# Decode attention beside a feed-forward: K loaded in pairs of tiles into two large buffers, V tile by tile into two others

## Chip, cores and metric

The kernel runs on one core of one Trainium2 chip. The metric is device time in microseconds (us) of one execution: 2529.17 us, the median of three runs (2528.84 to 2529.18). A DMA issue below is one instruction on the SP (SyncE) queue that moves one block from HBM to SBUF over the core's 16 DMA engines.

## Reference

One token `x` (512 numbers) goes through attention with a long cache and through a gated feed-forward, and a scalar gate mixes the two:

```python
g = sigmoid((x * gate_w).sum(-1))
q = (x @ wq)                                  # 32 heads of 128
scores = einsum("bhqd,bhkd->bhqk", q, k_cache) * 128 ** -0.5   # 65536 keys a head
a = einsum("bhqk,bhkd->bhqd", softmax(scores), v_cache) @ wo   # 4096 -> 512
b = (silu(x @ w_gate) * (x @ w_up)) @ w_down  # 512 -> 1792 -> 512
return g * a + (1 - g) * b
```

All inputs are bf16. `k_cache` and `v_cache` are 32 x 65536 x 128 each, 1.07 GB together; everything else is about 14 MB. Each cache entry is read once.

## The kernel before

**Tiles.** A head's 65536 keys are cut into G = 4 tiles of 16384 keys; over 32 heads that makes N = 128 K tiles and 128 V tiles. A tile is 128 partitions by 128 keys by 128 numbers, 32 KB a partition and 4 MB in all. Within a tile partition p holds 128 consecutive keys, so its 32 KB are one contiguous run in HBM (L110). `ring` has five slots of 32 KB a partition (L17, L81). `take` hands out the slot that has been free longest, `give` returns it; K, V, `wq`, the feed-forward's weights and the last half of `wo` all pass through these five. A load into a slot waits until the last reader of its earlier contents has finished.

**Queries.** All 32 heads' q are made at the start: 32 matmuls (L147) with `x` spread over 128 columns give q copied to all partitions, and ScalarE stores it as `q_bc` (L154).

**One K tile.** VectorE multiplies the tile by q (L245, in place) and halves the width by adding (L249): from 128 to 64 in the first G tiles, to 32 after those (`width_of`). TensorE finishes the sum over the remaining columns with matmuls by the identity into `S_ps` (`scores`, L258: 16 matmuls in the first four tiles, 8 after). VectorE sums the last four (`fold`, L272). After four tiles of a head, `row_max` (L278 to L282) and `exponentials` (L287 to L291) turn the scores into `P_sb`. In the first tile of each head the multiplication and the additions are done in two halves so that these small steps can go between.

**One V tile.** `values` (L313): 32 matmuls of 128x512 into `O_ps`. After a head's four V tiles, `head_turn` (L342, L349) brings the result into a column of `oT`, and `project` (L356) adds that head's row of `wo`. `wo` comes in four blocks of four heads (L161) along the way for heads 0 to 15, and in four pieces behind the last V tile (L167) for heads 16 to 31.

**Order.** The order on each engine is written out by hand (`manual_schedule`, the list `steps` at L397 and the loop at L408). Each step loads one K tile and one V tile (L410, L415), multiplies one K tile, runs `values` for one V tile and then `scores` for the K tile. V runs behind K by up to LAG = 8 tiles. All cache loads are issued on SP in the order of the loop, and SP stands still at a load whose slot is not free. The last V tile is loaded in six pieces (`V_CUTS`), and its last 8 key columns go through `head_turn` directly (L334).

Of the kernel before, what the change touches and what calls it, by code (L numbers as in the profile page):

```python
# [11 lines left out]
P = 128  # L12
# [4 lines left out]
SLOTS = 5  # L17
# [5 lines left out]
LAG = 8  # L23
SPREAD = 40

WG = 4
LATE = 16
LATE_CUTS = (0, 5, 10, 14, LATE)
TURNED = 8
V_CUTS = {3: (0, 64, NB), 2: (0, 64, NB), 1: (0, 32, 64, 96, 112, NB - TURNED, NB)}  # L30


@with_exitstack
def kernel(
# [26 lines left out]
    QG = 4  # L61
    assert Dh == P and Sk % (NB * P) == 0 and NBH <= 512 and H % QG == 0 and G >= 2
# [5 lines left out]
    ppool = ctx.enter_context(tc.tile_pool(name="ppool", bufs=3))  # L68
    wo_pool = ctx.enter_context(tc.tile_pool(name="wo_pool", bufs=2))
# [8 lines left out]
    free = list(range(SLOTS))  # L78
    held = {}

    def take(name):  # L81
        slot = free.pop(0)
        held[name] = slot
        return ring.tile(
            [P, NB * Dh], bf16, name=name.split(".")[0], tag=f"slot{slot}"
        )

    def give(name):
        free.append(held.pop(name))


    consts.tile([P, 32], bf16, name="fill")
# [5 lines left out]

    QW = QG * Dh
    wq_t = take("wq_t.0")  # L100
    nc.sync.dma_start(out=wq_t, in_=A_wq.rearrange("(p t) f -> p (t f)", t=KT))
    wq_sb = wq_t.rearrange("p (t f) -> p t f", t=KT)

    K_tiles, V_tiles, S_tiles, F_tiles, P_tiles, O_tiles = {}, {}, {}, {}, {}, {}

    def load(dst, cache, n, name, cuts=(0, NB)):
        h, g = divmod(n, G)
        t = take(f"{name}.{n}")
        view = t.rearrange("p (j d) -> p j d", d=Dh)
        src = cache[0, h, g * NB * P : (g + 1) * NB * P, :].rearrange("(p j) d -> p j d", j=NB)  # L110
        for a, b in zip(cuts[:-1], cuts[1:]):
            nc.sync.dma_start(out=view[:, a:b, :], in_=src[:, a:b, :])
        dst[n] = view

    def load_k(n):
        load(K_tiles, A_k_cache, n, "K_t")

    def load_v(n):
        load(V_tiles, A_v_cache, n, "V_t", V_CUTS.get(N - n, (0, NB)))

    for n in range(G):
        load_k(n)
# [8 lines left out]
    q_bc = consts.tile([P, H * Dh], bf16, name="q_bc")  # L131
    X_bc = consts.tile([P, KT, P], bf16, name="X_bc")
    for t in range(KT):
        nc.vector.tensor_copy(out=X_bc[:, t, :], in_=xT[:, t : t + 1].to_broadcast([P, P]))

    rowsum = consts.tile([P, H], f32, name="rowsum")
# [3 lines left out]
    b_sb = consts.tile([1, D], f32, name="b_sb")  # L140
# [3 lines left out]
    def queries(g):  # L144
        qg_ps = psum_m.tile([P, QW], f32, name="qg_ps", tag="misc")
        for t in range(KT):
            nc.tensor.matmul(  # L147
                qg_ps,
                lhsT=X_bc[:, t, :],
                rhs=wq_sb[:, t, g * QW : (g + 1) * QW],  # L150
                start=(t == 0),
                stop=(t == KT - 1),
            )
        nc.scalar.activation(out=q_bc[:, g * QW : (g + 1) * QW], in_=qg_ps, func=ACT.Copy)  # L154

    wo_tiles = {}

    def load_wo(g):
        wo_tiles[g] = wo_pool.tile([P, WG, D], bf16, name="wo_sb", tag="wo_sb")
        rows = A_wo[g * WG * P : (g + 1) * WG * P, :]  # L160
        nc.sync.dma_start(out=wo_tiles[g], in_=rows.rearrange("(h p) n -> p h n", p=P))  # L161

    def load_late(cuts):
        late = take("wo_late.0")[:, : LATE * D].rearrange("p (h n) -> p h n", n=D)
        rows = A_wo[(H - LATE) * P :, :].rearrange("(h p) n -> p h n", p=P)
        for a, b in zip(cuts[:-1], cuts[1:]):
            nc.sync.dma_start(out=late[:, a:b, :], in_=rows[:, a:b, :])  # L167
        return late
# [52 lines left out]
    def feed_forward_out(hT, rest):  # L221
        b_ps = psum_m.tile([1, D], f32, name="b_ps", tag="misc")
        for t in range(FT):
            nc.tensor.matmul(
                b_ps, lhsT=hT[:, t : t + 1], rhs=wd_sb[:, t, :], start=(t == 0), stop=(t == FT - 1)
            )
        nc.scalar.activation(out=b_sb, in_=b_ps, func=ACT.Copy, scale=rest)
        for i, a in enumerate(a_ps):
            nc.tensor.matmul(
                a, lhsT=ones_f[0:1, 0:1], rhs=b_sb[:, i * HD : (i + 1) * HD], start=True, stop=False  # L230
            )
# [4 lines left out]
    def products(n, a=0, b=NB):  # L236
        h = n // G
        K = K_tiles[n][:, a:b, :]
        qb = q_bc[:, h * Dh : (h + 1) * Dh]
        q_rep = bass.AP(  # L240
            tensor=qb.tensor,
            offset=qb.offset,
            ap=[list(qb.ap[0]), [0, b - a], [1, Dh]],
        )
        yield nc.vector.tensor_tensor(out=K, in0=K, in1=q_rep, op=ALU.mult)  # L245
        half = Dh
        while half > width_of(n):
            half //= 2
            yield nc.vector.tensor_tensor(  # L249
                out=K[:, :, 0:half], in0=K[:, :, 0:half], in1=K[:, :, half : 2 * half],  # L250
                op=ALU.add,
            )

    def scores(n):
# [11 lines left out]
        give(f"K_t.{n}")  # L266
# [18 lines left out]
    def exponentials(h, mT_ps):  # L285
# [4 lines left out]
        P_tiles[h] = ppool.tile([P, NBH], bf16, name="P_sb")  # L290
# [16 lines left out]
    def values(n):  # L307
# [12 lines left out]
        if n < N - 1:  # L320
            del V_tiles[n]
            give(f"V_t.{n}")

    def head_copy(h):
        O_sb = small.tile([4, 4 * Dh], f32, name="O_sb")
# [27 lines left out]
    def project(h):  # L353
        rows = wo_tiles[h // WG][:, h % WG, :] if h < H - LATE else wo_late[:, h - (H - LATE), :]
        for i, a in enumerate(a_ps):
# [3 lines left out]
                rhs=rows[:, i * HD : (i + 1) * HD],  # L359
# [5 lines left out]
    def score_tile(n):  # L365
        for _ in products(n):
            pass
        if n:
            fold(n - 1)

    for g in range(H // QG):
        queries(g)
    give("wq_t.0")
    gu_t = take("gu_t.0")
    wgu_sb = gu_t[:, : 2 * KT * F].rearrange("p (w t f) -> p w t f", w=2, t=KT)
    for w, rows in enumerate((B_w_gate, B_w_up)):
        nc.sync.dma_start(out=wgu_sb[:, w], in_=rows.rearrange("(p t) f -> p t f", t=KT))
    score_tile(0)
    xs = gate_sum()
    scores(0)  # L380
    eg2 = gate_exp(xs)
    wd_t = take("wd_t.0")
    wd_sb = wd_t[:, : FT * D].rearrange("p (t n) -> p t n", t=FT)
    nc.sync.dma_start(out=wd_sb, in_=B_w_down.rearrange("(p t) n -> p t n", t=FT))
    score_tile(1)
    rest = gate_value(eg2)
    scores(1)
    load_k(4)
    score_tile(2)
    scores(2)  # L390
    load_v(0)
    ff = feed_forward_in()
    give("gu_t.0")
    score_tile(3)
    scores(3)

    steps = []  # L397
    v = 0
    for n in range(G, N):
        due = not (n >= SPREAD and n % 4 == 3 and n - v < LAG)  # L400
        steps.append((n, v if due else None))
        v += due
    while v < N:
        steps.append((None, v))
        v += 1

    done = tot_ps = wo_late = None
    for n, v in steps:  # L408
        if n is not None and n > G:
            load_k(n)  # L410
        if v is not None:
            if v % (WG * G) == 2 and v // (WG * G) < (H - LATE) // WG:
                load_wo(v // (WG * G))
            if v:
                load_v(v)  # L415
            if v == N - 1:
                wo_late = load_late(LATE_CUTS)
        vector = iter(()) if n is None else products(n)
        top_of = None
        if n is None:  # L420
            top_of = H - 1 if F_tiles else None
        elif n % G == 0:
            top_of = n // G - 1
            vector = (i for a in (0, NB // 2) for i in products(n, a, a + NB // 2))
        if top_of is not None:
            next(vector, None)
            fold(top_of * G + G - 1)
            mT_ps = row_max(top_of)
            next(vector, None)
            exponentials(top_of, mT_ps)  # L430
        if n == G:
            hT = feed_forward_mid(*ff)
        for _ in vector:
            pass
        if n is not None and n % G:
            fold(n - 1)
        if tot_ps is not None:
            weight(*tot_ps)
            tot_ps = None
        if n == G:  # L440
            feed_forward_out(hT, rest)
            give("wd_t.0")
        if done is not None:
            head_turn(done, head_copy(done))
        if v is not None:
            values(v)
        if top_of is not None:
            tot_ps = top_of, total(top_of)
        if n is not None:
            scores(n)  # L450
        if done is not None and done < H - LATE:
            project(done)
        done = v // G if v is not None and v % G == G - 1 else None
    head_turn(H - 1, head_copy(H - 1))
    for h in range(H - LATE, H):
        project(h)

    out_sb = consts.tile([1, D], bf16, name="out_sb")
# [33 lines left out]
```

## Time and profile before

| what | value |
|---|---|
| median of three runs | 2529.17 us |
| the profiled execution's own time | 2529.15 us |
| its span in the trace | 2527.4 us |
| VectorE busy | 2083.6 us (82%) |
| TensorE matmuls busy | 1523.3 us (60%) |
| ScalarE busy | 77.6 us (3%) |
| DMA queue q1 (SP's) | 42,674 packets, 1087.65 MB |
| a whole K tile: issues, median us to landing | 128, 36.9 |
| a whole V tile: issues, median us to landing | 125, 29.2 |

The span runs from the first to the last instruction of the trace; 1.75 us of the execution's own time lie around it. "Busy" is the sum of an engine's instructions. The time to landing counts from the issue on SP's queue to the last byte, so it holds the wait behind the transfers that are queued ahead. A wait is put down to the event that came last.

### The profile page before, as it was taken

To read this page: it belongs to the slowest core of one execution; us is meant where nothing else is said; L and a number is where in the kernel's file an instruction comes from. 1 tells how busy PE (TensorE), PEld (TensorE's weight loads), DVE (VectorE), ACT (ScalarE), POOL (GpSimd) and SP (SyncE) were. 2 spreads that over 40 slices of the span, in tenths; PEclk is the share of its full clock that TensorE was granted. 3 is DMA by queue.
4 is the path that set the end of the run, shared out by engine and by line. 5 is a ranking of instruction groups with operands and counts; after the bars stand their busy time and mean duration, and the time that the engine had idled before them with its cause. 6 is when DMAs were issued, how large, how long until landed. Compare 5 with 4: busy or idle time off the path is not lost.

```text
span 2527.4 us, 13150 instructions
## 1 busy us (share of the span) xinstructions
PE 1523.3 (60%) x5770; PEld 579.9 (23%) x5770; DVE 2083.6 (82%) x744; ACT 77.6 (3%) x207; POOL 0.7 (0%) x6
## 2 busy tenths in 40 slices
PE   3666556655666555556665666566556665665568
PEld 1322222221222212212222222222222221222223
DVE  6988888788888999988888888888888888888860
ACT  1000000000000000000000000000000000000000
POOL 0000000000000000000000000000000000000000
PEclk7877777777777777787777777777877777777779
DMA  9999999999999999999999999999999999999998
GB/s 415 435 431 431 434 434 432 433 432 431 434 431 435 432 431 433 433 432 434 432 433 432 432 433 434 433 432 432 433 434 433 432 432 432 435 434 432 431 432 370
DMA packets 43019, 1088.49 MB, mean 431 GB/s; under 512 B 4689, under 2 KB 8786, under 8 KB 9170
## 3 DMA queue, kind: packets, MB, share of 16 engines
q1 hardware_dynamic: 42674, 1087.65, 99.9%
q8 instruction: 45, 0.74, 0.1%
q14 instruction: 12, 0.10, 0.0%
q10 hardware_dynamic: 288, 0.00, 0.0%
HBM read 1087.64 MB, written 0.00 MB: 430 GB/s over the span
## 4 chain that ended last, share of the span: by engine, by line
DMA 71%; PE 22%; DVE 6%; issue 0%; ACT 0%; SPq 0%; DVEq 0%
DMA V_t<-in_A_v_cache_dram 65%; PE O_ps L313 21%; DMA K_t<-in_A_k_cache_dram 6%; DVE K_t L245 3%; DVE K_t L249 2%; PE S_ps L258 1%; DMA wo_late<-in_A_wo_dram 0%; DVE S_sb L272 0%; PE oh_ps L342 0%; DVE m L278 0%; ACT P_sb L291 0%; PE a_ps L356 0%; PE mT_ps L282 0%; ACT O_sb L326 0%; DVE top L287 0%
## 5 line engine op out<-in xcount | busy, mean ns | idle before, releaser
L313 PE MATMUL O_ps<-V_t,P_sb 128*4 128x512 bf16 x4094 | 1149.9, 451 | 672.4 <-DMA V_t<-in_A_v_cache_dram 672.4
L245 DVE TENSOR_TENSOR K_t<-K_t,q_bc 128x16384 bf16<-128x16384 bf16 (+1 forms) x159 | 1117.2, 7026 | 346.0 <-DMA K_t<-in_A_k_cache_dram 346.0
L249 DVE TENSOR_TENSOR K_t<-K_t 128x8192 bf16<-128x8192 bf16 (+1 forms) x314 | 859.8, 2738 | 8.6
L313 PEld LDWEIGHTS <-P_sb 128*4 128x4 bf16 x4094 | 392.7, 97 | 1409.4 <-issue 1064.4
L258 PE MATMUL S_ps<-K_t,ident_b 128*128 128x512 bf16 x1056 | 265.3, 395 | 97.3 <-DVE K_t L249 97.1
L258 PEld LDWEIGHTS <-ident_b 128*128 128x128 bf16 x1056 | 98.6, 102 | 245.2 <-issue 156.0
L282 PE MATMUL mT_ps<-diag,ones_f 128*128 128x128 f32 x64 | 23.9, 473 | 141.3 <-ACT diag L280 141.3
L342 PE MATMUL oh_ps<-ident_f,O_sb 4*128 4x1 f32 x256 | 55.5, 334 | 74.5 <-ACT O_sb L326 74.5
L272 DVE TENSOR_REDUCE S_sb<-S_ps 128x128 f32<-128x512 f32 x128 | 87.5, 684 | 4.8 <-PE S_ps L258 4.8
L280 ACT ACTIVATE diag<-ident_f,m 128x128 f32<-128x128 f32 x32 | 12.8, 402 | 2110.1 <-DVE m L278 2110.1
L342 PEld LDWEIGHTS oh_ps<-ident_f,O_sb 4*128 4x128 f32 x256 | 52.8, 301 | 84.1 <-ACT O_sb L326 79.8
L282 PEld LDWEIGHTS mT_ps<-diag,ones_f 128*128 128x128 f32 x64 | 14.9, 289 | 158.4 <-ACT diag L280 158.4
L459 DVE CAST out_sb<-a_ps 1x256 bf16<-1x256 f32 x1 | 0.4, 411 | 58.3 <-PE a_ps L356 58.3
L291 ACT ACTIVATE P_sb<-S_sb,bias 128x512 bf16<-128x512 f32 x32 | 23.1, 722 | 1.0
L278 DVE TENSOR_REDUCE m<-S_sb 128x1 f32<-128x512 f32 x32 | 22.0, 686 | 1.1
L326 ACT ACTIVATE O_sb<-O_ps 4x512 f32<-4x512 f32 x32 | 18.3, 572 | 132.8 <-PE O_ps L313 132.8
L147 PE MATMUL qg_ps<-wq_t,X_bc 128*128 128x512 bf16 x32 | 8.8, 443 | 13.0 <-DMA wq_t<-in_A_wq_dram 13.0
L304 DVE RECIPROCAL recip<-tot_ps 128x1 f32<-128x1 f32 x32 | 5.1, 158 | 12.5 <-PE tot_ps L299 12.5
L299 PEld LDWEIGHTS tot_ps<-rowsum,ones_f 128*128 128x128 f32 x64 | 9.5, 188 | 14.0 <-issue 14.0
L299 PE MATMUL tot_ps<-rowsum,ones_f 128*128 128x1 f32 x64 | 12.2, 260 | 0.0
L349 ACT ACTIVATE oT<-oh_ps,rg 128x1 bf16<-128x1 f32 x32 | 8.4, 264 | 63.4 <-PE oh_ps L342 63.4
L287 DVE TENSOR_REDUCE top<-mT_ps 128x1 f32<-128x128 f32 x32 | 9.1, 284 | 1.0 <-PE mT_ps L282 1.0
(42 smaller groups left out, 68.9 us busy)
## 6 DMA issues: line engine op xcount, KB each, us to landing
K_t<-in_A_k_cache_dram SPq DMA_DIRECT2D x128, 4096.0 KB, 36.9
V_t<-in_A_v_cache_dram SPq DMA_DIRECT2D x125, 4096.0 KB, 29.2
V_t<-in_A_v_cache_dram SPq DMA_DIRECT2D x4, 2048.0 KB, 31.7
wq_t<-in_A_wq_dram SPq DMA_DIRECT2D x1, 4096.0 KB, 12.3
V_t<-in_A_v_cache_dram SPq DMA_DIRECT2D x3, 1024.0 KB, 32.1
wo_sb<-in_A_wo_dram SPq DMA_DIRECT2D x4, 512.0 KB, 33.8
gu_t<-in_B_w_gate_dram SPq DMA_DIRECT2D x1, 1792.0 KB, 34.3
gu_t<-in_B_w_up_dram SPq DMA_DIRECT2D x1, 1792.0 KB, 38.2
```

Of the source, the lines that this page charges most:

```text
L245: yield nc.vector.tensor_tensor(out=K, in0=K, in1=q_rep, op=ALU.mult)
L249: yield nc.vector.tensor_tensor(out=K[:, :, 0:half], in0=K[:, :, 0:half], in1=K[:, :, half : 2 * half], op=ALU.add,)
L258: nc.tensor.matmul(S, lhsT=ident_b, rhs=K_tiles[n][:, :, c : c + QUAD], start=(c == 0), stop=(c == width - QUAD),)
L272: nc.vector.tensor_reduce(out=S_tiles[h][:, g * NB : (g + 1) * NB], in_=F_tiles.pop(n), axis=AXIS.X, op=ALU.add)
L278: nc.vector.tensor_reduce(out=m, in_=S_tiles[h], axis=AXIS.X, op=ALU.max)
L280: nc.scalar.activation(out=diag, in_=ident_f, func=ACT.Copy, scale=m)
L282: nc.tensor.matmul(mT_ps, lhsT=ones_f, rhs=diag, start=True, stop=True)
L291: nc.scalar.activation(out=P_tiles[h], in_=S_tiles[h], func=ACT.Exp, bias=bias, scale=scale, accum_out=rowsum[:, h : h + 1],)
L299: nc.tensor.matmul(tot_ps, lhsT=ones_f, rhs=rowsum[:, h : h + 1], start=True, stop=True)
L313: nc.tensor.matmul(O_tiles[h], lhsT=P_tiles[h][:, g * NB + j : g * NB + j + 4], rhs=V_tiles[n][:, j : j + 4, :], start=(g == 0 and j == 0) ...
L326: nc.scalar.activation(out=O_sb, in_=O_tiles.pop(h), func=ACT.Copy)
L342: nc.tensor.matmul(oh_ps, lhsT=O_sb[:, c * Dh : (c + 1) * Dh], rhs=ident_f[0:4, c : c + 1], start=(c == 0 and not turned), stop=(c == 3),)
```

## The change

K tiles are loaded in pairs: two tiles of a head become one block of 128 partitions by 256 keys, 64 KB a partition, contiguous in HBM, in one DMA issue (the first and the last pair come in two). Two buffers of 64 KB a partition are for K alone, two of 32 KB for V alone. A V tile is half of such a block: 32 KB runs at a pitch of 64 KB. Which key stands in which partition changes accordingly, for K and V alike. A loop over the M = 64 pairs takes the place of the list of steps; a pair's slot comes free when `scores` of its second tile is done. `values` runs four tiles behind the K tile of the same loop turn, ahead of that tile's `scores`. q is made as 32 columns at the start (128 matmuls of one column) and spread to all partitions head by head (`query`). Heads 0 to 15 of `wo` load in one issue behind the last K pair, into the K buffer that has come free, and are projected in the last turn; the second halves of the two K buffers then take V tiles 124 and 127, and heads 16 to 31 of `wo` go beside the latter. The products of a head's first tile are no longer cut in halves. The core of the diff:

```diff
-SLOTS = 5
+PAIR = 2 * NB
+SLOTS = 2
+EARLY = 16
+LATE_CUTS = (EARLY, 21, 26, 30, 32)
...
-    free = list(range(SLOTS))
+    free = {kind: list(range(SLOTS)) for kind in "KV"}
...
+    def load(view, cache, m, cuts, start=0):
+        h, g = divmod(m, MH)
+        rows = cache[0, h, g * PAIR * P : (g + 1) * PAIR * P, :]
+        src = rows.rearrange("(p j) d -> p j d", j=PAIR)
         for a, b in zip(cuts[:-1], cuts[1:]):
+            nc.sync.dma_start(out=view[:, a:b, :], in_=src[:, start + a : start + b, :])
+    def load_k(m):
+        view = take(f"K_t.{m}", "K").rearrange("p (j d) -> p j d", d=Dh)
+        load(view, A_k_cache, m, (0, NB, PAIR) if m in (0, M - 1) else (0, PAIR))
+        for i in range(2):
+            K_tiles[2 * m + i] = view[:, i * NB : (i + 1) * NB, :]
...
+    def queries():
+        q_ps = psum_m.tile([P, H], f32, name="q_ps", tag="misc")
+        for h in range(H):
+            for t in range(KT):
+                nc.tensor.matmul(
+                    q_ps[:, h : h + 1],
+                    lhsT=wq_sb[:, t, h * Dh : (h + 1) * Dh],
+                    rhs=xT[:, t : t + 1],
+                    start=(t == 0), stop=(t == KT - 1),
+                )
+        nc.scalar.activation(out=qT, in_=q_ps, func=ACT.Copy)
+    def query(h):
+        diag = small.tile([P, P], bf16, name="q_diag")
+        nc.scalar.activation(out=diag, in_=ident_f, func=ACT.Copy, scale=qT[:, h : h + 1])
+        qb_ps = psum_m.tile([P, P], f32, name="qb_ps", tag="misc")
+        nc.tensor.matmul(qb_ps, lhsT=ones_b, rhs=diag, start=True, stop=True)
+        q_tiles[h] = small.tile([P, P], bf16, name="q_sb")
+        nc.scalar.activation(out=q_tiles[h], in_=qb_ps, func=ACT.Copy)
...
+    for i in range(M):
+        h, first = i // MH, i % MH == 0
+        vector = products(2 * i)
+        next(vector)
+        if mT_ps is not None:
+            exponentials(h - 1, mT_ps)
+        if not first:
+            fold(2 * i - 1)
+        for _ in vector:
+            pass
+        if i == M - 1:
+            for o in range(EARLY):
+                project(o)
+        if i >= 2:
+            values(2 * i - 4)
+            if i < M - 2:
+                load_v(2 * i - 2)
+            elif i == M - 1:
+                load_v(N - 3)
+        scores(2 * i)
...
+        if i >= 2:
+            values(2 * i - 3)
+            if i < M - 2:
+                load_v(2 * i - 1)
+            elif i == M - 1:
+                load_v(N - 2)
...
+        if first and i > MH:
+            head_turn(h - 2, head_copy(h - 2))
+        vector = products(2 * i + 1)
+        next(vector)
+        fold(2 * i)
...
+        scores(2 * i + 1)
...
+        if i + 2 < M:
+            load_k(i + 2)
+        elif i + 2 == M:
+            spare = take("wo_early.0", "K")
+            wo_sb = load_wo(spare, (0, EARLY))
+            load_v(N - 6)
+            load_v(N - 5)
+            load_v(N - 4, spare)
+        if not first:
+            fold(2 * i + 1)
+            mT_ps = row_max(h)
+    spare = take("wo_late.0", "K")
+    load_v(N - 1, spare)
+    exponentials(H - 1, mT_ps)
+    tot_ps = total(H - 1)
+    head_turn(H - 2, head_copy(H - 2))
+    values(N - 4)
+    values(N - 3)
+    weight(H - 1, tot_ps)
+    wo_sb = load_wo(spare, LATE_CUTS)
+    values(N - 2)
+    values(N - 1)
     head_turn(H - 1, head_copy(H - 1))
+    for h in range(EARLY, H):
         project(h)
```

More of the change, by code (lines that the diff above doesn't have):

```diff
@@ L21 @@
 WIDTH = 32
[L23 to L28, printed above, removed]
 TURNED = 8
 V_CUTS = {3: (0, 64, NB), 2: (0, 64, NB), 1: (0, 32, 64, 96, 112, NB - TURNED, NB)}
+EARLY = 16
+LATE_CUTS = (EARLY, 21, 26, 30, 32)
 @with_exitstack
@@ L60 @@
     N = H * G
-    QG = 4
-    assert Dh == P and Sk % (NB * P) == 0 and NBH <= 512 and H % QG == 0 and G >= 2
+    M = N // 2
+    MH = G // 2
+    assert Dh == P and G == 4 and NBH == 512 and H * D <= PAIR * Dh
     scale = float(Dh) ** -0.5
@@ L67 @@
     small = ctx.enter_context(tc.tile_pool(name="small", bufs=2))
-    ppool = ctx.enter_context(tc.tile_pool(name="ppool", bufs=3))
-    wo_pool = ctx.enter_context(tc.tile_pool(name="wo_pool", bufs=2))
     psum_s = ctx.enter_context(tc.tile_pool(name="psum_s", bufs=2, space=bass.MemoryType.PSUM))
@@ L75, with take @@
     ctx.enter_context(tc.manual_schedule())
-    free = list(range(SLOTS))
+    free = {kind: list(range(SLOTS)) for kind in "KV"}
     held = {}
-    def take(name):
-        slot = free.pop(0)
-        held[name] = slot
+    def take(name, kind):
+        slot = free[kind].pop(0)
+        held[name] = kind, slot
         return ring.tile(
-            [P, NB * Dh], bf16, name=name.split(".")[0], tag=f"slot{slot}"
+            [P, (PAIR if kind == "K" else NB) * Dh], bf16,
+            name=name.split(".")[0], tag=f"{kind}{slot}",
         )
     def give(name):
-        free.append(held.pop(name))
-    consts.tile([P, 32], bf16, name="fill")
+        kind, slot = held.pop(name)
+        free[kind].append(slot)
+    consts.tile([P, 96], bf16, name="fill")
     xT = consts.tile([P, KT], bf16, name="xT")
@@ L97, with load_v @@
         nc.scalar.dma_start(out=gwT, in_=gate_w.rearrange("(p t) -> p t", t=KT))
[L99 to L110, printed above, removed]
-        for a, b in zip(cuts[:-1], cuts[1:]):
[L112 to L122, printed above, removed]
+    wq_t = take("wq_t.0", "V")
+    nc.sync.dma_start(
+        out=wq_t[:, : KT * H * Dh], in_=A_wq.rearrange("(p t) f -> p (t f)", t=KT)
+    )
+    wq_sb = wq_t[:, : KT * H * Dh].rearrange("p (t f) -> p t f", t=KT)
+    K_tiles, V_tiles, S_tiles, F_tiles, P_tiles, O_tiles, q_tiles = {}, {}, {}, {}, {}, {}, {}
+    def load(view, cache, m, cuts, start=0):
+        h, g = divmod(m, MH)
+        rows = cache[0, h, g * PAIR * P : (g + 1) * PAIR * P, :]
+        src = rows.rearrange("(p j) d -> p j d", j=PAIR)
+        for a, b in zip(cuts[:-1], cuts[1:]):
+            nc.sync.dma_start(out=view[:, a:b, :], in_=src[:, start + a : start + b, :])
[4 more added lines that the diff above has]
+            K_tiles[2 * m + i] = view[:, i * NB : (i + 1) * NB, :]
+    def load_v(n, spare=None):
+        if spare is None:
+            view = take(f"V_t.{n}", "V")
+        else:
+            view = spare[:, NB * Dh :]
+        V_tiles[n] = view = view.rearrange("p (j d) -> p j d", d=Dh)
+        load(view, A_v_cache, n // 2, V_CUTS.get(N - n, (0, NB)), n % 2 * NB)
+    load_k(0)
+    load_k(1)
     ident_f = consts.tile([P, P], f32, name="ident_f")
@@ L129 @@
     nc.vector.memset(ones_f, 1.0)
[L131 to L134, printed above, removed]
+    ones_b = consts.tile([P, P], bf16, name="ones_b")
+    nc.vector.memset(ones_b, 1.0)
+    qT = consts.tile([P, H], f32, name="qT")
     rowsum = consts.tile([P, H], f32, name="rowsum")
@@ L139 @@
     rg = consts.tile([P, H], f32, name="rg")
-    b_sb = consts.tile([1, D], f32, name="b_sb")
     HD = D // 2
     a_ps = [psum_a.tile([1, HD], f32, name=f"a{i}_ps") for i in range(2)]
[L144 to L165, printed above, removed]
+    def queries():
[6 more added lines that the diff above has]
+                    rhs=xT[:, t : t + 1],
+                    start=(t == 0),
+                    stop=(t == KT - 1),
+                )
+        nc.scalar.activation(out=qT, in_=q_ps, func=ACT.Copy)
@@ new lines, in query, with load_wo @@
+    def query(h):
[5 more added lines that the diff above has]
+        nc.scalar.activation(out=q_tiles[h], in_=qb_ps, func=ACT.Copy)
+    def load_wo(tile, cuts):
+        t = tile[:, : H * D].rearrange("p (h n) -> p h n", n=D)
+        rows = A_wo.rearrange("(h p) n -> p h n", p=P)
@@ L166, in load_late @@
         for a, b in zip(cuts[:-1], cuts[1:]):
-            nc.sync.dma_start(out=late[:, a:b, :], in_=rows[:, a:b, :])
-        return late
+            nc.sync.dma_start(out=t[:, a:b, :], in_=rows[:, a:b, :])
+        return t
     def feed_forward_in():
@@ L226, in feed_forward_out @@
             )
+        b_sb = small.tile([1, D], f32, name="b_sb", tag="row", bufs=1)
         nc.scalar.activation(out=b_sb, in_=b_ps, func=ACT.Copy, scale=rest)
@@ L234, in width_of, with products @@
         return FIRST if n < G else WIDTH
[L236 to L239, printed above, removed]
+    def products(n):
+        K = K_tiles[n]
+        qb = q_tiles[n // G][:, :]
         q_rep = bass.AP(
-            tensor=qb.tensor,
-            offset=qb.offset,
-            ap=[list(qb.ap[0]), [0, b - a], [1, Dh]],
+            tensor=qb.tensor, offset=qb.offset, ap=[list(qb.ap[0]), [0, NB], [1, Dh]]
         )
@@ L265, in scores @@
         del K_tiles[n]
-        give(f"K_t.{n}")
+        if n % 2:
+            give(f"K_t.{n // 2}")
     def fold(n):
@@ L289, in exponentials @@
         nc.scalar.activation(out=bias, in_=top, func=ACT.Copy, scale=-scale)
-        P_tiles[h] = ppool.tile([P, NBH], bf16, name="P_sb")
+        P_tiles[h] = small.tile([P, NBH], bf16, name="P_sb")
         nc.scalar.activation(
@@ L319, in values @@
             )
-        if n < N - 1:
-            del V_tiles[n]
+        if f"V_t.{n}" in held:
             give(f"V_t.{n}")
     def head_copy(h):
-        O_sb = small.tile([4, 4 * Dh], f32, name="O_sb")
+        O_sb = small.tile([4, 4 * Dh], f32, name="O_sb", tag="row", bufs=1)
         nc.scalar.activation(out=O_sb, in_=O_tiles.pop(h), func=ACT.Copy)
@@ L353, in project @@
     def project(h):
-        rows = wo_tiles[h // WG][:, h % WG, :] if h < H - LATE else wo_late[:, h - (H - LATE), :]
         for i, a in enumerate(a_ps):
@@ L358, in project @@
                 lhsT=oT[:, h : h + 1],
-                rhs=rows[:, i * HD : (i + 1) * HD],
+                rhs=wo_sb[:, h, i * HD : (i + 1) * HD],
                 start=False,
@@ L362, in project @@
             )
[L365 to L372, printed above, removed]
+    queries()
     give("wq_t.0")
-    gu_t = take("gu_t.0")
+    wd_t = take("wd_t.0", "V")
+    gu_t = take("gu_t.0", "V")
     wgu_sb = gu_t[:, : 2 * KT * F].rearrange("p (w t f) -> p w t f", w=2, t=KT)
+    wd_sb = wd_t[:, : FT * D].rearrange("p (t n) -> p t n", t=FT)
     for w, rows in enumerate((B_w_gate, B_w_up)):
@@ L377 @@
         nc.sync.dma_start(out=wgu_sb[:, w], in_=rows.rearrange("(p t) f -> p t f", t=KT))
[L378 to L383, printed above, removed]
-    nc.sync.dma_start(out=wd_sb, in_=B_w_down.rearrange("(p t) n -> p t n", t=FT))
[L385 to L432, printed above, removed]
@@ L433 @@
+    nc.sync.dma_start(out=wd_sb, in_=B_w_down.rearrange("(p t) n -> p t n", t=FT))
+    query(0)
+    mT_ps = tot_ps = None
+    for i in range(M):
[6 more added lines that the diff above has]
+            fold(2 * i - 1)
         for _ in vector:
             pass
-        if n is not None and n % G:
-            fold(n - 1)
+        if i == M - 1:
[8 more added lines that the diff above has]
+        scores(2 * i)
+        if i == 0:
+            xs = gate_sum()
+            eg2 = gate_exp(xs)
+        if i >= 2:
[4 more added lines that the diff above has]
+                load_v(N - 2)
+        if mT_ps is not None:
+            tot_ps = total(h - 1)
+            mT_ps = None
+        if first and i > MH:
[3 more added lines that the diff above has]
+        fold(2 * i)
+        if i == 1:
+            hT = feed_forward_mid(*ff)
+            feed_forward_out(hT, rest)
+            give("gu_t.0")
+            load_v(0)
+            give("wd_t.0")
+            load_v(1)
+        for _ in vector:
+            pass
+        if i == 0:
+            rest = gate_value(eg2)
@@ L437 @@
         if tot_ps is not None:
-            weight(*tot_ps)
+            weight(h - 1, tot_ps)
             tot_ps = None
[L440 to L452, printed above, removed]
@@ L453 @@
-        done = v // G if v is not None and v % G == G - 1 else None
+        if not first and h + 1 < H:
+            query(h + 1)
+        scores(2 * i + 1)
+        if i == 0:
+            ff = feed_forward_in()
+        if i + 2 < M:
[9 more added lines that the diff above has]
+            mT_ps = row_max(h)
@@ L454 @@
+    spare = take("wo_late.0", "K")
[9 more added lines that the diff above has]
+    values(N - 1)
     head_turn(H - 1, head_copy(H - 1))
-    for h in range(H - LATE, H):
+    for h in range(EARLY, H):
         project(h)
-    out_sb = consts.tile([1, D], bf16, name="out_sb")
+    out_sb = small.tile([1, D], bf16, name="out_sb", bufs=1)
```

## The prediction, as it stood before the changed kernel ran

> **What bounds the kernel now.** I read the page's DMA rows first, then VectorE's rows in time in the middle of the run, then the chain of waits over the last 100 us. The page:
>
> ```profile
> GB/s 415 435 431 431 434 434 432 433 432 431 434 431 435 432 431 433 433 432 434 432 433 432 432 433 434 433 432 432 433 434 433 432 432 432 435 434 432 431 432 370
> q1 hardware_dynamic: 42674, 1087.65, 99.9%
> ```
>
> SP's queue keeps all 16 DMA engines busy for the whole span, at 431 to 435 GB/s in every slice but the first and the last. VectorE in time, in the middle:
>
> ```profile
> 1537.56 8.69 DVE L245 TENSOR_TENSOR K_t<-K_t,q_bc 128x16384 bf16<-128x16384 bf16 x1 [2.27 <-DMA K_t<-in_A_k_cache_dram]
> 1546.29 6.75 DVE L249 TENSOR_TENSOR K_t<-K_t 128x8192 bf16<-128x8192 bf16 x2
> 1552.96 0.68 DVE L272 TENSOR_REDUCE S_sb<-S_ps 128x128 f32<-128x512 f32 x1
> ...
> 1556.90 8.69 DVE L245 TENSOR_TENSOR K_t<-K_t,q_bc 128x16384 bf16<-128x16384 bf16 x1 [2.99 <-DMA K_t<-in_A_k_cache_dram]
> ```
>
> A K tile costs VectorE 16.1 us, then it waits for the next to land. Landings are 19.34 us apart, for one K and one V tile: 8.39 MB, 434 GB/s. So the bytes set the pace and the other engines have room. The chain at the end:
>
> ```profile
> 2511.18 12.15 DMA wo_late<-in_A_wo_dram
> 2523.33 0.04 issue
> 2523.37 1.48 PE a_ps L356 x12
> ```
>
> The run ends on a transfer too: the last piece of `wo` lands at 2523.33, and 4.07 us later the span (2527.4) is over. Three things can therefore move the time: the cost of moving the same bytes, a queue that runs dry, and the work left after the last landing.
>
> **Cost of the bytes.** The trace's records of single packets give the starts on one DMA engine: two 32 KB packets (one partition of one tile) begin 1209.5 ns apart, 16 KB 607, 14 KB 532, 8 KB 306, 1 KB 42. That is a straight line, 27.2 bytes a ns plus 4.7 ns a packet. Each issue adds one 4-byte landing mark an engine, 6 ns. K has 128 x 128 / 16 = 1024 packets an engine before. After, 62 pairs come as 64 KB rows (62 x 8 = 496 packets) and two pairs in halves (32), so 496 are gone: 496 x 4.7 ns = 2.33 us. 62 fewer K issues and 3 fewer of `wo` save 65 x 6 ns = 0.39 us. V, the weights and the pieces of the last V tile keep their packets. Sum: **-2.7 us**. No row shows a 64 KB packet; its bounds are one packet free of overhead (2409 ns, -5.2 us with the issues) and two of 32 KB (2419 ns, -0.4 us). I take the line, which holds from 1 to 32 KB.
>
> Here two rules of the Trainium skill speak, both in "DMA: Bandwidth & Descriptors". In "Anatomy of one DMA" a transfer (on GpSimd's path) costs about 2.0 us plus its bytes. If that stood in series, 62 fewer transfers would give 124 us. The landings above speak against it: two issues of 4 MB in 19.34 us are all bytes. In "Latency and other measured facts" large power-of-two row pitches slow HBM copies: 207 instead of 214 GB/s at 512 KiB, half at 4 MiB. The pitch here goes from 32 KB to 64 KB, so by that rule an estimate is no loss; the same 3.3% would be 82 us.
>
> **The queue.** *Middle.* Count from the landing of a pair, with 38.7 us (two K, two V tiles) to the next. VectorE needs 2 x (8.69 + 6.75 + 0.68) = 32.2 us plus some 1 us of row maximum and weights. TensorE runs `values` on V tiles that land at 9.7 and 19.3 (8.6 us each after idling), each with the 1.9 us of `scores` behind it, so the second tile's `scores` end near 34. Then the pair's slot is free, while the next pair (until 38.7) and two V tiles (until 58.1) still stand ahead of its load: 24 us of cover. V slots come free near 18 and 28, 20 us ahead of need. The spread of q adds two small ScalarE operations (0.4 us, as L280) and one 128x128 matmul a head, on engines that are 3% and 60% busy. Cost 0.
>
> *Start.* Nothing but `wq`, two pairs and the feed-forward's weights is queued until the first pair is used up: 5 x 9.68 + 24 x 0.532 = 61.1 us, from 3.1 on (the first packet begins at 2.1 and takes 1.0 longer than the rest), so dry at 64.2; with 1.3 us from issue to first packet the third pair must be issued by 62.9.
>
> ```profile
> 13.04 8.78 PE L147 MATMUL qg_ps<-wq_t,X_bc 128*128 128x512 bf16 x32 [13.04 <-DMA wq_t<-in_A_wq_dram]
> 22.82 8.69 DVE L245 TENSOR_TENSOR K_t<-K_t,q_bc 128x16384 bf16<-128x16384 bf16 x1 [14.03 <-DMA K_t<-in_A_k_cache_dram]
> 55.32 0.33 SPq L112 DMA_DIRECT2D K_t<-in_A_k_cache_dram  x1
> 69.01 6.83 PE L176 MATMUL gu_ps<-xT,gu_t 128*128 128x1 bf16 x112
> ```
>
> Before, the slot of tile 1 was reused 32.5 us after the first product. The new 128 one-column matmuls cost 61 ns each by L176 (7.8 us), or twice that while TensorE is as slow as in the first 3.4 us of L147 (its first eight matmuls are 0.43 us apart, later ones 0.215). With 3.4 us slow they end at 22.5, and 1.5 us for a copy (0.2, L184), the diagonal (0.4), one matmul (0.5, L282) and a copy (0.3, L127) put the first product at 24.0 (22.8 to 30.2). The third pair's issue is then at 56.5 (55.3 to 62.7). Cost 0, with 6 us of cover; without it, 1 us for each us late. *Behind the last pair*, `wo`'s first half needs the slot of pair 62, free near 34, due at 38.7 - 1.3: 3 us of cover, cost 0.
>
> **The end.** Let 0 be the landing of the last K pair. The queue then brings heads 0 to 15 of `wo` (128 packets of 42 ns an engine: 5.4 us), six V tiles (9.7 each) and `wo`'s rest (5.4): it lands at 69.0. As a check, before: nine V tiles and the rest of `wo` are 92.7 us by this count; from the last K landing at 2430.99 to 2523.33 it took 92.3. If the transfer still came last, the end would be at 69.0 + 4.1 = 73.1.
>
> TensorE, though, has to go through its own order. It projects 16 heads when `wo` has landed (5.4), done near 10. `values` of tile 122 wait for its landing at 15.1 and stand *ahead* of the `scores` of K tile 126. VectorE has multiplied tile 127 by 18.2 and waits there in `fold` of 126. From here everything is a chain; its durations are these rows and L272, L249, L258 above:
>
> ```profile
> 2440.67 8.40 PE L313 MATMUL O_ps<-V_t,P_sb 128*4 128x512 bf16 x32 [7.97 <-DMA V_t<-in_A_v_cache_dram]
> ...
> 2449.01 1.90 PE L258 MATMUL S_ps<-K_t,ident_b 128*128 128x512 bf16 x8
> 2450.95 0.69 DVE L272 TENSOR_REDUCE S_sb<-S_ps 128x128 f32<-128x512 f32 x1 [3.87 <-PE S_ps L258]
> ...
> 2465.74 0.30 PEld L299 LDWEIGHTS tot_ps<-rowsum,ones_f 128*128 128x128 f32 x2 [0.44 <-issue]
> ...
> 2466.05 20.88 PE L313 MATMUL O_ps<-V_t,P_sb 128*4 128x512 bf16 x96
> ```
>
> `values` 122 end at 23.5, `scores` 126 at 25.5, `fold` and the two additions at 33.0, `scores` 127 at 34.9. From there to the end of the next V tile took 15.1 us before (2450.95 to 2466.05: softmax, total, turning a head, `values`): 50.0. Tiles 125 and 126 at 96 matmuls in 20.88 us, 6.96 each: 63.9. The 30 matmuls of tile 127: 70.4, though its last piece has landed at 63.7. From the last of these to the end of the span took 8.1 us before (2519.26 to 2527.4: the last columns, turning the head, 32 matmuls of `project` at 0.11, the output): 78.5. That is 78.5 - 73.1 = **+5.4 us** against a queue that ends last. Bounds: 0 (the transfer still ends last) and 7.9 (`values` 122 and 124 as slow as the slowest such rows in the middle, 9.65 and 9.93).
>
> **Sum.** 2529.15 - 2.7 + 5.4 = 2531.9 us, from the profiled execution's own time, which is the median of the three runs to 0.02. A measurement of this kernel can tell about 0.2% (5 us) from no change; this is 0.11%.
>
> **Rivals.**
> 1. *Forecast* (0.50): one packet a row, TensorE late by 5.4 at the end: 2531.9. For it: the straight line, and the order of the queue behind the last pair.
> 2. *A 64 KB row moves as two packets* (0.19), so the change doesn't do what it could: only 0.4 is saved, 2529.15 - 0.4 + 5.4 = 2534.2, at the edge of slower: at the end's upper bound 2536.7. The point is a row that takes 2 x 1209.5 ns again while the end costs over 5.4. For it: no row over 32 KB in the trace; against: the line shows no limit yet.
> 3. *The end is hidden* (0.12): `scores` 126 run before tile 122 lands, or TensorE catches up: 2526.5. Against: the order in the code.
> 4. *The queue runs dry* (0.08): the first product as late as 30.2 plus a late landing of the weights, or pair 62 freed 3 us late. Some 2 to 6 us: 2534 to 2538.
> 5. *The pitch* (0.05), the second rule above: HBM answers rows 64 KB apart more slowly. Each 1% of the 256 tiles' 2478 us is 25 us: 2557. Against: rows 1, 14 and 32 KB long lie on one line.
> 6. *K packets cost nothing at all and all engines end level* (0.06): -5.2, the end hidden, and the 1.8 us by which the engines' mean is ahead of the last (their last marks are at 2520.07 to 2523.67): 2522.
>
> **Numbers.** Faster by over 0.2% (below 2524.1): case 6, 0.06. Slower (above 2534.2): 0.03 of case 1, 0.13 of case 2, 0.07 of 4 and 0.05 of 5: 0.28. Within: 0.66. The range 2526.0 to 2537.5 takes in cases 1 to 3 and most of 4; some 0.13 is left out.
>
> **What would show it.** The packet count: 42,674 - 16 x 496 - 16 x 65, about 33,700, and K issues of 8192 KB. `O_ps` after the last V landing without a wait, and a chain whose last steps are L313's successor, `head_turn` and `project` with no transfer of `wo` among them; VectorE waiting some 7 us for `S_ps` once, some 60 us before the end. Wrong if slices in the middle leave 431 to 435, if the third pair's issue comes after 63 us, or if the chain still ends on `wo_late`.

## The result, and the profile after

The changed kernel takes 2532.44 us (median of 19 runs, 2531.23 to 2534.19), the kernel before 2529.08 us (19 runs, 2528.84 to 2529.38). The ratio is 1.0014, 95% interval [1.0008, 1.0020]: slower by 3.4 us, clear of noise and less than the 0.2% named above. The forecast was 2531.9.

The profiled execution is the fastest of the 19: 2531.23 us, span 2529.4 us, so 2.1 us above the profiled execution before. The page's rows on the transfers:

```profile
DMA  9999999999999999999999999999999999999998
GB/s 415 434 443 425 432 436 433 435 432 431 439 426 433 437 430 435 441 425 437 430 433 440 427 433 438 428 437 429 434 435 435 431 435 430 439 436 424 437 403 358
q1 hardware_dynamic: 33698, 1087.65, 99.6%
```

SP's queue moved the same 1087.65 MB in 33,698 packets instead of 42,674. That is the 16 x 496 packets and 16 x 65 landing marks that were to go, to the packet: a 64 KB row is one packet (7,936 packets of 65,536 bytes in the records). The slices in the middle leave 431 to 435 (424 to 443), which the prediction had named as a sign of being wrong. They do not show a slower or a dry queue there: their mean is 433.4, against 432.7 before, and in e9 below, which has K in 32 KB rows again, they are 431 to 436. A larger packet falls into one slice or the next. The two last slices are lower than before (403 and 358 against 432 and 370).

The chain of waits over the last 70 us, where it ended on a piece of `wo` before:

```profile
2452.40 24.64 DMA V_t<-in_A_v_cache_dram
2477.05 0.04 issue
2477.09 7.07 PE O_ps L319 x32
2484.16 1.85 PE S_ps L263 x8
...
2489.01 0.82 ACT P_sb L297 x2
2489.83 0.04 issue
2489.88 0.59 PE tot_ps L305 x2
2490.47 1.79 PE oh_ps L347 x8
2492.26 29.25 PE O_ps L319 x126
...
2523.28 3.60 PE a_ps L360 x32
```

The last transfer on the path is a V tile that lands at 2477.05. From there it is TensorE with the softmax of the last head between; no transfer of `wo` comes after. The 126 matmuls of `values` for tiles 124 to 127 follow each other without a wait, although their tiles are there: TensorE is late, not the queue. The trace's landing records say by how much. The last piece of `wo` lands 2.4 us earlier than before (2521.51 against 2523.95, on the clock of the views), and the span ends 7.9 us after it instead of 3.4.

VectorE's rows in time show the wait that starts this:

```profile
2454.20 6.74 DVE L254 TENSOR_TENSOR K_t<-K_t 128x8192 bf16<-128x8192 bf16 x2
...
2460.86 8.68 DVE L250 TENSOR_TENSOR K_t<-K_t,q_sb 128x16384 bf16<-128x16384 bf16 x1
2467.42 7.07 PE L319 MATMUL O_ps<-V_t,P_sb 128*4 128x512 bf16 x32 [3.94 <-DMA V_t<-in_A_v_cache_dram]
2474.42 1.90 PE L263 MATMUL S_ps<-K_t,ident_b 128*128 128x512 bf16 x8
...
2476.36 0.69 DVE L278 TENSOR_REDUCE S_sb<-S_ps 128x128 f32<-128x512 f32 x1 [6.81 <-PE S_ps L263]
2476.97 6.74 DVE L254 TENSOR_TENSOR K_t<-K_t 128x8192 bf16<-128x8192 bf16 x2
```

VectorE has multiplied the last K tile by 2469.5 and stands 6.81 us for the `scores` of the tile before it. These were ready to run since 2460.9, when its additions ended, but in TensorE's order they come behind `values` of V tile 122, which wait for that tile until 2467.42.

One more place differs, the end of the last K pair. The busy time by stretch (span, then PE, PEld, DVE, ACT, POOL, the granted clock of TensorE, the DMA share, GB/s):

```profile
2435.00:2443.00 8.00, 7.82 (x41) 3.73 (x39) 7.97 (x4) 0.15 (x1) 0.00 (x0) 1.00 0.98 422
2443.00:2451.00 8.00, 3.50 (x8) 1.07 (x8) 7.96 (x4) 0.12 (x1) 0.00 (x0) 0.79 0.57 234
2451.00:2459.00 8.00, 1.26 (x7) 0.75 (x7) 7.97 (x4) 0.00 (x0) 0.00 (x0) 0.55 1.10 419
```

For 8 us the DMA engines are busy 57% of the time: the queue is dry on some of them. By the durations in the packet records the idle time between 2440 and 2455 is 3.2 us an engine in the mean. Whether it costs anything is one of the questions below.

### The profile page after: what moved, and what is told of

Its sections match the earlier page's. It is cut to its first block, busy times and chain, and to the rows that moved or that the text cites. A ratio compares the mean times of both kernels' runs of the same rounds, so it can differ in the third digit from the quotient of the medians.

```text
span 2529.4 us, 13204 instructions
## 1 busy us (share of the span) xinstructions
PE 1462.9 (58%) x5898; PEld 552.2 (22%) x5898; DVE 2063.4 (82%) x648; ACT 90.7 (4%) x264; POOL 0.7 (0%) x6
## 3 DMA queue, kind: packets, MB, share of 16 engines
q1 hardware_dynamic: 33698, 1087.65, 99.6%
## 4 chain that ended last, share of the span: by engine, by line
DMA 53%; DVE 40%; PE 6%; issue 0%; SPq 0%; ACT 0%; another core or an unknown queue 0%; DVEq 0%; ACTq 0%
DMA K_t<-in_A_k_cache_dram 52%; DVE K_t L250 23%; DVE K_t L254 17%; PE S_ps L263 4%; PE O_ps L319 1%; DMA V_t<-in_A_v_cache_dram 1%; DVE S_sb L278 1%; DVE top L293 0%; PE b_ps L231 0%; PE a_ps L360 0%; SPq L112 0%; PE oh_ps L347 0%; PE a_ps L237 0%; ACT P_sb L297 0%
## 5 line engine op out<-in xcount | busy, mean ns | idle before, releaser
L319 PE MATMUL O_ps<-V_t,P_sb 128*4 128x512 bf16 x4032 | 1020.1, 417 | 756.2 <-DMA V_t<-in_A_v_cache_dram 417.3
L250 DVE TENSOR_TENSOR K_t<-K_t,q_sb 128x16384 bf16<-128x16384 bf16 x128 | 1112.1, 8688 | 297.4 <-DMA K_t<-in_A_k_cache_dram 297.4
L254 DVE TENSOR_TENSOR K_t<-K_t 128x8192 bf16<-128x8192 bf16 x252 | 849.3, 3370 | 4.3
L319 PEld LDWEIGHTS <-P_sb 128*4 128x4 bf16 x4094 | 365.5, 91 | 1422.2 <-issue 657.8
L263 PE MATMUL S_ps<-K_t,ident_b 128*128 128x512 bf16 x1056 | 341.7, 480 | 215.3 <-DVE K_t L254 215.3
L263 PEld LDWEIGHTS <-ident_b 128*128 128x128 bf16 x1056 | 113.5, 112 | 397.3 <-issue 340.8
L168 ACT ACTIVATE q_sb<-qb_ps 128x128 bf16<-128x128 f32 x32 | 8.9, 277 | 1121.0 <-PE qb_ps L166 1121.0
L347 PE MATMUL oh_ps<-ident_f,O_sb 4*128 4x1 f32 x256 | 34.3, 251 | 0.5 <-ACT O_sb L331 0.5
L347 PEld LDWEIGHTS oh_ps<-ident_f,O_sb 4*128 4x128 f32 x256 | 31.6, 190 | 1.0 <-ACT O_sb L331 0.5
L164 ACT ACTIVATE q_diag<-ident_f,qT 128x128 bf16<-128x128 f32 x32 | 12.5, 391 | 0.0
```

The source lines that it names most:

```text
L254: yield nc.vector.tensor_tensor(out=K[:, :, 0:half], in0=K[:, :, 0:half], in1=K[:, :, half : 2 * half], op=ALU.add,)
L263: nc.tensor.matmul(S, lhsT=ident_b, rhs=K_tiles[n][:, :, c : c + QUAD], start=(c == 0), stop=(c == width - QUAD),)
L319: nc.tensor.matmul(O_tiles[h], lhsT=P_tiles[h][:, g * NB + j : g * NB + j + 4], rhs=V_tiles[n][:, j : j + 4, :], start=(g == 0 and j == 0) ...
L347: nc.tensor.matmul(oh_ps, lhsT=O_sb[:, c * Dh : (c + 1) * Dh], rhs=ident_f[0:4, c : c + 1], start=(c == 0 and not turned), stop=(c == 3),)
```

## The experiments

**Theory A**, from the prediction: the queue sets the pace and a packet costs its engine 4.7 ns beside its bytes, so the pairs save 2.7 us; what is lost, and more, is lost behind the last landing, where TensorE's order is too long. **Theory B**: the dry stretch costs its 3.2 us and TensorE's order nothing. **Theory C**: packets cost nothing, the bytes alone count. All runs were timed beside the kernel before, on four chips (its medians are 2529.06 to 2529.11); "last landing" is the last landing of `wo`'s last piece in the trace's records.

**e1: `scores` ahead of `values` in the last turn of the loop.** The loads keep their order.

```diff
+        if i == M - 1:
+            scores(2 * i)
         if i >= 2:
             values(2 * i - 4)
...
-        scores(2 * i)
+        if i < M - 1:
+            scores(2 * i)
...
-        if i >= 2:
+        if 2 <= i < M - 1:
             values(2 * i - 3)
...
         scores(2 * i + 1)
+        if i == M - 1:
+            values(2 * i - 3)
+            load_v(N - 2)
```

> In the last turn of the loop, scores of K tile 126 stand ahead of values of V tile 122, and scores of 127 ahead of values of 123; all loads keep their order. Theory A (TensorE's order at the end costs 4 us; the 64 KB rows save 2.7): the fold of tile 126 waits no longer, the run ends on the last piece of wo again, some 4 us earlier than the changed kernel: 2528.3 us (2527 to 2529). Theory B (what costs is the stretch without transfers behind the last K pair, 51.7 engine-us or 3.2 us in the mean of 16 engines, and TensorE's order nothing): this stretch stays, so no change, 2532.4.

Measured: 2528.78 us (2526.57 to 2530.88), 3.7 below the changed kernel, ratio to before 0.9998 [0.9989, 1.0007]. The dry stretch is still there (2.45 us an engine), so B is out as the main cause. But the run does not end on `wo`: the span ends 5.8 us after the last landing (2521.82). VectorE now goes through without a wait until 2476.8, and `values` of 123 (7 us), placed behind `scores` of 127, hold up the softmax's matmul by 5 us: its input is there at 2482.2, and it starts at 2487.3. A was right in size and too simple in the mechanism.

**e2: every K pair in two issues of 32 KB rows**, `(0, NB, PAIR)` for all pairs.

> Every K pair comes in two issues of 32 KB rows instead of one of 64 KB rows; buffers and order stay. Theory A: 496 more packets an engine at 4.7 ns and 62 more issues at 6 ns, +2.7 us on the changed kernel: 2535.1. The first half of pair 62 also lands 9.7 us earlier, so the stretch without transfers behind the last K pair should go, for nothing. Theory B: that stretch was worth 3.2 us: 2532.4 + 2.7 - 3.2 = 2531.9. Theory C (packets are hidden and only bytes count): 2532.4.

Measured: 2535.21 us (2533.83 to 2535.80), +2.8; the last landing is at 2523.99, as before the change. The dry stretch shrank from 3.2 to 1.15 us an engine. A holds, B and C do not. This run still ends on TensorE, 9.7 us after the last landing, so the price of the rows is shown more cleanly by e8 and e9.

**e3: V tiles 122 and 123 load ahead of `wo`'s first half**, and the 16 projections move behind `scores` of tile 127.

```diff
-            if i < M - 2:
+            if i < M - 1:
                 load_v(2 * i - 2)
...
-            if i < M - 2:
+            if i < M - 1:
                 load_v(2 * i - 1)
...
             wo_sb = load_wo(spare, (0, EARLY))
-            load_v(N - 6)
-            load_v(N - 5)
             load_v(N - 4, spare)
```

> V tiles 122 and 123 load ahead of the first half of wo, so the queue has 19 us of V behind the last K pair, and values of 122 can start 5.4 us earlier; the 16 projections move behind scores of tile 127. Theory A: TensorE's chain starts 5.4 us earlier and the run ends on wo's last piece: 2528.3 us, as in e1 (within 0.5). Theory B: the stretch without transfers goes, 3.2 us: 2529.2. If both cost, this one is below e1 by the share of the dry stretch.

Measured: 2527.72 us (2526.51 to 2528.24), ratio 0.9994 [0.9985, 1.0002]. The queue is dry for 0.06 us an engine instead of 3.2, and the last landing moves from 2521.51 to 2521.11: the stretch was worth 0.4 us there (0.3 by e4, e6 and e8, which lack it too and land at 2521.2). It hit the engines that were ahead. The 16 engines' landings of the last K piece in the changed kernel lie 9 us apart (2443.0 to 2452.2), and the last engine had its next packets in time.

**e4: e1 and e3 together.**

> e1 and e3 together. Theory A: the end is hidden in either alone, so nothing is added: 2528.3 at most, and 2526.4 (before less the 2.7 of the packets) at best if the dry stretch also costs the slowest engine something in most executions. Theory B: 2529.2. Below 2529.1 it beats both kernels.

Measured: 2533.94 us (2532.84 to 2534.32). Both theories missed by 5 us. The last landing is at 2521.2, as in e3, but the span ends 11.3 us after it. TensorE in time:

```profile
2476.69 3.36 PE L263 MATMUL S_ps<-K_t,ident_b 128*128 128x512 bf16 x8 [4.46 <-DVE K_t L254]
2479.99 7.07 PE L319 MATMUL O_ps<-V_t,P_sb 128*4 128x512 bf16 x32
...
2486.89 3.66 PE L360 MATMUL a_ps<-wo_early,oT 128*1 128x256 bf16 x32
...
2494.30 9.96 PE L319 MATMUL O_ps<-wo_early,P_sb 128*4 128x512 bf16 x32
2504.10 13.98 PE L319 MATMUL O_ps<-V_t,P_sb 128*4 128x512 bf16 x64
```

Between `scores` of the last K tile (end 2480.05) and the softmax's 0.5 us matmul, which can only begin at 2490.5, stand `values` of 123 and the 16 projections: 10.5 us of work that could wait. `values` of 124 start at 2494.3, where e3 has them at 2489.6. So theory A stays with a sharper statement: the path to the end is `scores` of the last K tile, the softmax's small matmul, then four V tiles; whatever TensorE has between the first two is on it.

**e7: the changed kernel with the 16 projections behind `values` of tile 124**, from ahead of `values` of 122, where TensorE waits anyway.

> The changed kernel with one edit: the 16 projections stand behind values of V tile 124 instead of ahead of values of tile 122. The transfers are the same. Theory A (from the landing of V tile 122 on, every instruction of TensorE is on the path to the end): 32 matmuls of 0.11, +3.6 us: 2536.0. If a transfer set the end: no change, 2532.4.

Measured: 2536.34 us (2535.38 to 2536.84), +3.9. TensorE's work behind the last softmax is on the path: in the trace the 32 matmuls stand there with 3.5 us. That they make up all of the 3.9 is not shown, since `values` of 122, now after 19.3 us of standing still, took 9.10 us in this trace instead of 7.07.

**e5: the kernel before with K tiles in two issues of 16 KB rows**, a cut of `(0, NB // 2, NB)` in its `load_k`: the suspected packet cost by itself, in a kernel whose end the transfers set (in this run's trace the span ends 3.4 us after the last landing, as before).

> The kernel before with every K tile in two issues of 16 KB rows. Theory A (each packet costs 4.7 ns on its DMA engine, each issue 6 ns): 1024 more packets an engine and 128 more issues, 4.8 + 0.8 = +5.6 us: 2534.7. Theory C (packets are hidden, only bytes count, and the 2.5 us by which the changed kernel's last transfer lands earlier come from the new order of the loads): 2529.1.

Measured: 2534.55 us (2534.41 to 2534.74), +5.5, ratio 1.0022 [1.0013, 1.0030]. Theory C is out.

**e6: e3's loads, `scores` of 126 first, the projections behind `values` of 124.**

> The changed kernel with V tiles 122 and 123 ahead of the first half of wo (as e3), scores of K tile 126 ahead of values of V tile 122 (as e1), and the 16 projections behind values of tile 124, so that nothing stands between scores of tile 127 and the softmax's matmul. Theory A: P_sb is ready near 2485 us, before V tile 124 lands (2486.6); the run ends on wo's last piece (2521.1) as before the change, 3.5 to 4 us before the end of the span: 2526.4 us (2526.0 to 2527.2), with a spread of the runs like the 0.8 us of the kernel before. If TensorE's order were not the cause of the spread and the loss, it would stay at 2527.7, as e3.

Measured: 2529.43 us (2528.41 to 2531.09); the expectation missed by 3. `P_sb` was ready in time, but the projections were now on the path themselves: `values` of 124 end at 2496.1, 32 matmuls of `project` take until 2499.6, and V tile 125 had landed by then.

**e8: e6 with the projections in the two gaps**, 8 heads ahead of the softmax's matmul and 8 behind it:

```diff
         scores(2 * i + 1)
+        if i == M - 1:
+            for o in range(EARLY // 2):
+                project(o)
...
             mT_ps = row_max(h)
+            if i == M - 1:
+                for o in range(EARLY // 2, EARLY):
+                    project(o)
```

> e6 with the 16 projections in two halves: 8 heads between scores of tile 127 and the softmax's matmul, 8 between that matmul and total. In e6 TensorE stood still in just these two places (2481.4 to 2483.3 and 2483.8 to 2485.25), 3.35 us, and the projections took 3.5 us on the path behind values of tile 124. Theory A: values of tile 124 start near 2487 and end near 2494, before V tile 125 lands (2496); from there the transfers set the end, and the last landing is 3.5 to 4 us before the end of the span: 2526.5 us (2526.0 to 2527.2), below both kernels, with runs as close together as those of the kernel before. If something else than these 3.5 us holds the end up, it stays at 2527.7 (e3) or above.

Measured: 2526.55 us (2526.39 to 2526.94), ratio 0.9990 [0.9981, 0.9999]: faster than both kernels, 2.5 us below the one before. TensorE in time and the end of the chain of waits:

```profile
2479.36 1.91 PE L263 MATMUL S_ps<-K_t,ident_b 128*128 128x512 bf16 x8
2481.20 1.91 PE L360 MATMUL a_ps<-wo_early,oT 128*1 128x256 bf16 x16
2483.21 0.49 PE L288 MATMUL mT_ps<-diag,ones_f 128*128 128x128 f32 x2
2483.63 1.91 PE L360 MATMUL a_ps<-wo_early,oT 128*1 128x256 bf16 x16
...
2486.76 7.07 PE L319 MATMUL O_ps<-wo_early,P_sb 128*4 128x512 bf16 x32
```

```profile
2509.36 11.24 DMA wo_late<-in_A_wo_dram
2520.60 0.04 issue
2520.64 1.49 PE a_ps L360 x12
```

The projections fill the places where TensorE would wait for VectorE and ScalarE, `values` of 124 take 7.07 us instead of e6's 8.54, and the chain ends on `wo_late` as before the change: same 12 matmuls behind it, but at 2520.60 instead of 2523.33, 2.73 us earlier.

**e9: e8 with K in 32 KB rows.**

> e8 with every K pair in two issues of 32 KB rows, all else the same: the transfers set its end, so the rows' size is seen alone. Theory A (4.7 ns a packet, 6 ns an issue): +2.7 us, 2529.2, the time of the kernel before, so that pairs, buffers, order and the spread of q cost nothing together. Theory C (the bytes alone count): 2526.5.

Measured: 2529.25 us (2529.05 to 2529.51), ratio 1.0000 [0.9991, 1.0009]. Its chain:

```profile
2512.90 10.57 DMA wo_late<-in_A_wo_dram
2523.47 0.04 issue
2523.52 1.48 PE a_ps L360 x12
```

The piece of `wo` that the 12 matmuls wait for lands at 2523.47, against 2523.33 in the kernel before. So buffers, order and spread of q together cost nothing as long as the end is hidden, and the 2.7 us between e8 and e9 are the size of the rows, packets and issues together.

## Why the prediction was right, point by point

- **What bounds.** Right. In every run whose end is hidden the time follows the last landing, and that follows packets and bytes.
- **Cost of the bytes, -2.7 us.** Right: one packet a row; in the records two 64 KB packets begin 2414 ns apart on an engine, as the line had it (65536 / 27.2 + 4.7). The last landing came 2.4 us earlier in the changed kernel and 2.8 in e8; e9 takes it back (+2.7), e5 doubles it (+5.5 of 5.6).
- **The two rules of the Trainium skill** ("DMA: Bandwidth & Descriptors"). The fixed 2.0 us of "Anatomy of one DMA", stated for GpSimd's path, would have given 124 us for 62 fewer issues if they stood in series; e8 against e9, which differ in these 62 issues and their rows alone, gives 2.7. The loss at large row pitches ("Latency and other measured facts", stated from 512 KiB up) does not show at 64 KB: V's 32 KB packets, read at a pitch of 64 KB, begin 1209.5 ns apart as before.
- **The middle, 0.** Right. e9, with every part of the change but the rows' size and with a hidden end, takes the time of before.
- **The start, 0.** Right, by more than was counted: the 128 one-column matmuls took 3.57 us, not 9.5, because each was 28 ns, less than half of what L176 had shown. That the first product began at 24.16 (forecast 24.0) is luck, though: q was there at 18.0, and the product waited for its K tile, one of whose 16 engines landed at 24.1 when the others were done by 22.9. The third pair was issued at 57.0 (forecast 56.5).
- **Behind the last pair, "3 us of cover, cost 0".** The cover was wrong, the cost nearly right. The load was issued at 2448.4, when the first engines had been idle for 5 us: the count went from the landing, which is the last engine's, and the engines are up to 9 us apart. In addition the `scores` that free the slot took 3.5 us, not 1.9. It cost 0.4 us (e3), since the last engine was not among the idle ones.
- **The end, +5.4 us.** The mechanism was right: TensorE's order, `values` of 122 ahead of `scores` of 126, VectorE standing (6.81 us, "some 7"), a chain to the end with no `wo` in it. In the profiled run the end cost 7.9 - 3.4 = 4.5 us. `values` of 122 took 7.07 us there, not 8.40; they took 9.10 in e7 and 8.73 in e2, so the matmuls' speed after an idle time is one term that varies from run to run. One step of the chain was left out: `scores` of 127 waited for `values` of 123 (until 2484.1), 0.4 us longer than for VectorE's additions. One row was misread: 2523.33 is the landing of the third of the four late pieces of `wo`, the fourth landed at 2523.95, under the matmuls of the third, so the tail behind the last landing is 3.4 us and not 4.1. The median of the runs lies 3.4 us above before; with 2.4 gained by the transfers that leaves 5.8 for the end, against 5.4. That the forecast came within 0.5 us of the median is in part luck, as the runs themselves spread over 3.0 us.
- **Rivals.** Two packets a row (2534.2) is refuted by the packet count; the hidden end (2526.5) did not happen, but is what e8 reaches (2526.55); the dry queue happened and cost an eighth of what it looked like (0.4 of 3.2 us); the pitch cost nothing. That K's packets cost nothing at all (2522) is refuted by the 2414 ns, where the bytes alone are 2409, and by e8, which hides the end and still takes 2526.55.

## What to carry to other kernels

Where the transfers set the pace, look at what stands between the last landing and the end as closely as at the transfers: 2.7 us gained over the whole run were lost twice over by the order of a few dozen TensorE instructions in the last 70 us. In such an end find the small operations that others wait for (here one matmul of 0.5 us in the softmax) and let nothing stand ahead of them that could run later or in a gap. And count a buffer's cover from the first DMA engine that runs out for the idle time, but from the last one for the cost.

## What the runs showed of the hardware

- A DMA engine spends 4.7 ns on a packet beside its bytes at 27.2 bytes a ns: the six row sizes in the traces (1, 8, 14, 16, 32 and 64 KB; 42, 306, 532, 607, 1209.5 and 2414 ns from start to start) lie on this line.
- The 16 engines do not stay together: the landings of one 4 MB piece lay 9 us apart. In both traces packets that begin about 0.9 us late stand beside 16 KB packets on the instruction queue (45 or 46 of them). That these spread the engines fits the times, but was not tried.
- Kernels whose end was set by a transfer repeat within 0.6 us (the kernel before in its first 19 runs, e5, e8, e9); those that ended on TensorE spread by 1.5 to 4.3 us (the changed kernel 3.0, e1 4.3, e3 1.7). The same 32 matmuls of `values` took 7.07 to 9.96 us in these ends, and the granted clock of TensorE goes with it: tile 122 in the changed kernel 7.07 us at 1.00, tile 124 there 9.02 at 0.78, tile 124 in e4 9.96 at 0.70. That the spread of the runs comes from this is likely and not shown: each kernel left one trace.
- One-column matmuls with a new 128x128 weight took 28 ns each at the start (128 in 3.57 us, weight loads of 104 ns) and 61 ns at L176 before (weight loads of 159 ns); the feed-forward's, unchanged, took 63 ns after (56 in 3.52 us). The columns of `wq` lie side by side, those of the feed-forward's weights 14 apart; that this makes the difference is likely and was not tried.
